# Key-sum reciprocals as logarithm and exponential on ScalarE, and the first layer norm applied by GpSimd from tile 4 on, in a two-layer linear-attention and gated-unit kernel

## The chip, the cores and the metric

One NeuronCore of a Trainium2 chip. Its engines run their own instruction streams side by side: TensorE (PE) multiplies matrices, VectorE (DVE) and ScalarE (ACT) do elementwise work, GpSimd (POOL) does slower elementwise work, and SyncE (SP) issues most of the transfers. The metric is the device time of one execution in microseconds (us); lower is better.

## The reference

The input x has 2048 rows (positions) of 512 values in bf16. Four blocks follow, each added to x after a layer norm: attention, gated unit, attention, gated unit, with the same weights in both rounds.

```
A(x):  q, k, v = split(x @ wqkv), 32 heads of 16
       pq = q @ w_phi[head],  pk = k @ w_phi[head]
       phi = [softmax(p), softmax(-p)]          # 32 features per head, for q and for k
       kv  = sum over positions of phi_k^T v,   z = sum over positions of phi_k
       o   = (phi_q @ kv) / (phi_q . z + 1e-6)
       return o @ wo
B(x):  gate = x @ W_gate, up = x @ W_up          # 1376 columns
       return (relu(gate) * up) @ W_down
x = x + A(ln(x)); x = x + B(ln(x)); x = x + A(ln(x)); x = x + B(ln(x))
```

The softmax runs over 16 values, so for the keys each row of 128 positions needs 64 sums of exponentials (32 heads, two signs) and their 64 reciprocals.

## The kernel before, in words

All of x stays on the chip in `x_sb`, as 16 tiles of 128 rows. The layers are numbered l = 0 to 3: 0 and 2 are attention, 1 and 3 the gated unit. The work of a tile:

- `ln(l, ts)`: for each tile of a group VectorE takes the statistics (`stats`, L558, and their mean and variance `mv`, L559); ScalarE makes `rstd` for the whole group by a logarithm and an exponential (L561, L563); VectorE writes the normalised tile `y` (L572), from a ring of four buffers `p_y`. SyncE then transposes `y` into `yT` by a transfer (L587), or for a few tiles (`PE_Y`) TensorE does, with a copy by ScalarE (L581, L584). In layer 0 the groups are tiles 0, 1, 2, 3, (4, 5), (6, 7), (8 to 11), (12 to 15); elsewhere each tile is its own group.
- `kv_tile(l, t)`: TensorE multiplies `yT` with the composed key weights (L605), ScalarE writes exp(k) and exp(-k) into `phik` (L610), VectorE sums them in groups of 16 into `z`, 64 values (L611), takes the reciprocal `rz` (L613) and multiplies `phik` by it (L614). TensorE makes the values (L623), which ScalarE copies to `vaug` (L626).
- `q_chunk`: queries of four tiles (L639) and their exponentials `expq` (L643). `kv_sums`: the sums over all positions (L659), which need every tile's normalised `phik`; they are masked by VectorE into `kvs` (L667, L670).
- `attn_tile`: product with `kvs` (L692), denominators in `sm` by ScalarE and GpSimd (L706 to L717), VectorE's division and addition (L726, L731, L735), transposed `o`, product with `wo` (L752), addition to x (L755).
- `glu_slab` and `down`: gate and up products (L782), relu on ScalarE (L789), product on VectorE (L790), remainder columns (L810 on), down product (L834, L836), addition to x (L840).

The order of the instructions of each engine is not written by hand. Each `op(...)` names its engine, what it reads and writes, how long it holds its engine (`ii`) and its latency (`lat`), both in ns. `schedule` plans all operations by these figures, in eight rounds of a forward list schedule with priorities from a backward one; `prepare` turns the dependences into semaphore waits, and the engines run the planned orders as fixed queues. A waiting instruction holds up everything behind it on its engine. Buffers come from rings (`Pool`), and the planner also decides which tile has which buffer. When an operation is moved or its figures change, all the orders are planned anew.

ScalarE loads one table of functions at the start, `natural_log_exp_and_others`, and keeps it.

Of the kernel before, what the change touches and what calls it, by code (L numbers as in the profile page):

```python
# [5 lines left out]
FP32 = mybir.dt.float32  # L6
BF16 = mybir.dt.bfloat16
ALU = mybir.AluOpType
ACT = mybir.ActivationFunctionType
# [40 lines left out]
class Program:  # L50
# [8 lines left out]
    def op(self, eng, fn, reads=(), writes=(), parts=(), ii=100.0, lat=None, name="", claims=(), after=(), dma=None, nbytes=0):  # L59


        o = Op()
        o.i, o.eng, o.fn, o.name = len(self.ops), eng, fn, name
        o.ii, o.lat = float(ii), float(ii if lat is None else lat)
        o.dma, o.nbytes = dma, nbytes
        deps, order = set(), set()
        for a in after:
            (order if a.eng == eng else deps).add(a.i)

        def need(d, r):  # L70
            if d is o:
                return
            pe = r.tile is not None and r.tile.pool.psum and d.eng == "pe" and eng == "pe"
            (order if pe else deps).add(d.i)
        for r in reads:
            for w in r.writers:
                need(w, r)
        for r in writes:
            for u in r.writers + r.readers:
                need(u, r)  # L80
        for r in parts:
            for u in r.readers:
                need(u, r)
        for r in reads:
            r.readers.append(o)
        for r in writes:
            r.writers, r.readers = [o], []
        for r in parts:
            r.writers.append(o)
        o.uses = [r.tile for r in dict.fromkeys(list(reads) + list(writes) + list(parts)) if r.tile is not None]  # L90
        o.uses = list(dict.fromkeys(o.uses))
        o.tiles = list(dict.fromkeys(o.uses + list(claims)))
        for t in o.tiles:
            t.users.append(o)
        o.deps, o.order = sorted(deps), sorted(order - deps)
        o.cnt = o.stream = None
        self.ops.append(o)
        return o
# [279 lines left out]
def build_kernel(nc, A_x, A_wqkv, A_w_phi, A_wo, B_x, B_W_gate, B_W_up, B_W_down, out):  # L378
    pr = Program()
    op = pr.op  # L380
# [6 lines left out]
    def sb(name, shape, dt=BF16):  # L387
        return E(nc.sbuf_tensor(name, [P] + list(shape), dt))
# [5 lines left out]
    NT, NS, NC, FC = 16, 4, 4, 10  # L394
    x_sb = sb("x_sb", [NT, 512])
# [8 lines left out]
    mask2 = sb("mask2", [8])  # L404
    eps = sb("eps", [1], FP32)
    kvs = sb("kvs", [8, 144])
    stats, mv, lnv, rstd = sb("stats", [NT, 6], FP32), sb("mv", [NT, 2], FP32), sb("lnv", [NT, 1], FP32), sb("rstd", [NT, 1], FP32)

    p_y = ring("y", 4, [512])
# [24 lines left out]
    def tile(pool, *key):  # L434
        t = Tile(str(key), pool)
        return t, Res(str(key), t)
# [52 lines left out]
    for ic in range(4):  # L489
        t, r = tile(p_hT, "wkn", ic)  # L490
# [25 lines left out]
    for a in range(4):  # L516
        op("dve", lambda e, a=a: e.tensor_tensor(BD[:].rearrange("p c (a f b) -> p c a f b", f=16, b=2)[:, :, a], w128[:].unsqueeze(3).to_broadcast([P, 4, 16, 2]),
                                                 m8[:, 2 * a:2 * a + 2].unsqueeze(1).unsqueeze(1).to_broadcast([P, 4, 16, 2]), ALU.mult),
           reads=[c_w128, c_m8], writes=[c_BD[a]], ii=190, lat=280, name="BD")
# [35 lines left out]
    def ln(l, ts):  # L555

        for t in ts:
            op("dve", lambda e, t=t: e.bn_stats(stats[:, t, :], x_sb[:, t, :]), reads=[res("x", t)], writes=[res("st", t)], ii=600, lat=690, name=f"stat{l}.{t}")  # L558
            op("dve", lambda e, t=t: e.bn_aggr(mv[:, t, :], stats[:, t, :]), reads=[res("st", t)], writes=[res("mv", t)], ii=70, lat=175, name=f"aggr{l}.{t}")  # L559
        a, b = ts[0], ts[-1] + 1  # L560
        op("act", lambda e: e.activation(lnv[:, a:b, :], mv[:, a:b, 1:2], ACT.Ln, bias=eps[:]), reads=[res("mv", t) for t in ts] + [c_eps],  # L561
           writes=[res("lnv", t) for t in ts], ii=186, lat=295, name=f"ln{l}.{a}")
        op("act", lambda e: e.activation(rstd[:, a:b, :], lnv[:, a:b, :], ACT.Exp, scale=-0.5), reads=[res("lnv", t) for t in ts],  # L563
           writes=[res("rstd", t) for t in ts], ii=94, lat=203, name=f"rstd{l}.{a}")
        for t in ts:
            s = t // 4
            if (l, s) not in yT:
                yT[l, s] = Tile(f"yT{l}.{s}", p_yT)
            dst = yT[l, s]
            rr = res("yT", l, t, tile=dst)  # L570
            yt, yr = tile(p_y, "y", l, t)
            op("dve", lambda e, t=t, yt=yt: e.tensor_scalar(yt.ap(), x_sb[:, t, :], mv[:, t, 0:1], rstd[:, t, :], ALU.subtract, ALU.mult),  # L572
               reads=[res("x", t), res("mv", t), res("rstd", t)], writes=[yr], claims=[dst], ii=323, lat=405, name=f"y{l}.{t}")
            c = (t % 4) * 128
            if (l, t) in PE_Y:
                pt, pres = tile(p_ps, "yps", l, t)

                def mm(e, yt=yt, pt=pt):
                    b16 = pt.ap().bitcast(BF16)
                    for k in range(4):  # L580
                        i = e.transpose(b16[:, k * 128:(k + 1) * 128], yt.ap()[:, k * 128:(k + 1) * 128], ident[:])  # L581
                    return i
                op("pe", mm, reads=[yr] + c_id, writes=[pres], ii=230, lat=400, name=f"yT{l}.{t}")
                op("act", lambda e, pt=pt, dst=dst, c=c: e.activation(dst.ap()[:, :, c:c + 128], pt.ap().bitcast(BF16)[:, 0:512].rearrange("p (k n) -> p k n", k=4), ACT.Copy),  # L584
                   reads=[pres], writes=[rr], ii=477, lat=600, name=f"yTcp{l}.{t}")
            else:
                op("sp", lambda e, yt=yt, dst=dst, c=c: e.dma_start_transpose(dst.ap()[:, :, c:c + 128], yt.ap()), reads=[yr], writes=[rr],  # L587
                   dma="tr", nbytes=131072, name=f"yT{l}.{t}")
# [5 lines left out]
    def kv_tile(l, t):  # L594
        src, rr = yT[l, t // 4], res("yT", l, t)
        c0 = (t % 4) * 128
        kt, kr = tile(p_ps, "K", l, t)
        ft, fr = tile(p_ph, "ph", l, t)
        zt, zr = tile(p_z, "z", l, t)
        rt, rzr = tile(p_rz, "rz", l, t)  # L600
        ph[l, t] = (ft, fr)

        def mmk(e):
            for ic in range(4):
                i = e.matmul(kt.ap(), src.ap()[:, ic, c0:c0 + 128], Wkp[:, ic, :], start=(ic == 0), stop=(ic == 3))  # L605
            return i
        kop[l, t] = op("pe", mmk, reads=[rr] + r_wk, writes=[kr], claims=[ft], ii=864, lat=1030, name=f"K{l}.{t}")
        fr2 = [Res("phh", ft), Res("phh", ft)]
        for s in range(2):
            op("act", lambda e, s=s: e.activation(ft.ap()[:, s, :], kt.ap(), ACT.Exp, scale=(1.0, -1.0)[s]), reads=[kr], writes=[fr2[s]], ii=477, lat=600, name=f"expk{l}.{t}")  # L610
        op("dve", lambda e: e.tensor_reduce(zt.ap().rearrange("p (a b) -> p a b", b=2), ft.ap().rearrange("p s (a f b) -> p (s a) b f", f=16, b=2), AX.X, ALU.add),  # L611
           reads=fr2, writes=[zr], ii=1105, lat=1185, name=f"Z{l}.{t}")
        op("dve", lambda e: e.reciprocal(rt.ap(), zt.ap()), reads=[zr], writes=[rzr], ii=420, lat=526, name=f"rZ{l}.{t}")  # L613
        op("dve", lambda e: e.tensor_tensor(ft.ap().rearrange("p s (a f b) -> p (s a) f b", f=16, b=2), ft.ap().rearrange("p s (a f b) -> p (s a) f b", f=16, b=2),  # L614
                                            rt.ap().rearrange("p (a b) -> p a b", b=2).unsqueeze(2).to_broadcast([P, 32, 16, 2]), ALU.mult),
           reads=fr2 + [rzr], writes=[fr], ii=602, lat=695, name=f"norm{l}.{t}")
        vt, vr = tile(p_ps, "V", l, t)
        at, ar = tile(p_va, "va", l, t)
        va[l, t] = (at, ar)

        def mmv(e):
            for ic in range(4):
                i = e.matmul(vt.ap(), src.ap()[:, ic, c0:c0 + 128], wv[:, ic, :], start=(ic == 0), stop=(ic == 3))  # L623
            return i
        op("pe", mmv, reads=[rr, c_wv], writes=[vr], claims=[at], ii=864, lat=1030, name=f"V{l}.{t}")
        op("act", lambda e: e.activation(at.ap()[:, :, 0:128], vt.ap().rearrange("p (c n) -> p c n", c=4), ACT.Copy),  # L626
           reads=[vr] + ([res("va1", i) for i in range(16)] if l == 0 else []), writes=[ar], ii=477, lat=600, name=f"va{l}.{t}")
# [219 lines left out]
    for t in range(NT):  # L847
        kv_tile(0, t)
# [12 lines left out]
    for l in (0, 2):  # L861
# [7 lines left out]
        for s in range(NS):  # L869
# [3 lines left out]
            for t in range(4 * s, 4 * s + 4):  # L873
                down(l + 1, t, last=(l == 2))
                if l == 0:
                    ln(2, [t])
                    kv_tile(2, t)
    pr.schedule(ROUNDS)
    pr.prepare()
# [15 lines left out]


ROUNDS = 8
PE_Y = {(0, 0), (0, 1), (0, 2), (1, 0), (1, 1), (2, 15), (3, 0), (3, 1)}
PE_O = {(0, 0), (0, 1), (2, 0), (2, 1)}

# [42 lines left out]
```

## Time and profile before

| | |
|---|---|
| median of 3 runs | 408.67 us (406.94 to 409.31) |
| profiled execution | 408.02 us |
| its span, first to last instruction | 406.2 us |
| TensorE busy | 386.3 us (95%) |
| VectorE busy | 297.2 us (73%) |
| ScalarE busy | 194.1 us (48%) |
| GpSimd busy | 31.8 us (8%) |

In the profile's lines, L with a number is a line of the kernel, `out<-in` are the program's names for what an operation writes and reads, and xN is a count. A row of a timeline begins with its start and its length in us and ends, in square brackets, with the idle time before it and what ended it. A row of the waits is engine, operation and what it waited for, then total us, times and the longest. A row of the table by stretches has the stretch, its length, and then for TensorE's matmuls, TensorE's weight loads, VectorE, ScalarE and GpSimd the busy us and the number of instructions; behind them stand the clock that was granted to TensorE (1.00 is full speed), the share of the DMA engines and GB/s. A row of a group ends with total us and mean ns of one, then the idle time before.

### The profile page before, as it was taken

Reading aid. Unit: us, or ns where it says so; the run is one execution under the profiler, and the core shown is the slowest. Engines: PE = TensorE matmul, PEld = TensorE weight load, DVE = VectorE, ACT = ScalarE, POOL = GpSimd, SP = SyncE. Lnnn points to the kernel's source line nnn. Section 1 sums busy time; section 2 is a strip of 40 time slices with the busy share of each in tenths; the row PEclk is TensorE's granted clock in tenths of the full one; section 3 lists DMA queues with packets and bytes.
Section 4 is the critical chain, followed back from the end, with each engine's and each line's share of the span. In section 5 each row is a group of like instructions: output and inputs, shape, how many; then the busy total and the mean of one; then the engine's idle time right before and its main releaser. Section 6 shows DMA issues by size and latency. Waiting matters only on the chain.

```text
span 406.2 us, 6510 instructions
## 1 busy us (share of the span) xinstructions
PE 386.3 (95%) x2405; PEld 210.6 (52%) x2405; DVE 297.2 (73%) x635; ACT 194.1 (48%) x567; POOL 31.8 (8%) x119
## 2 busy tenths in 40 slices
PE   5869969999999999999999999989999999999996
PEld 2424645577845454444444466557765544444442
DVE  8989994699888855536499999499988872424424
ACT  4949518966554332323228964985554421203300
POOL 1000001221211000000000000222111200000000
PEclk9969969999999999999999999999999999999999
DMA  8655920133232220101104000013423231100012
GB/s 220 156 80 130 346 71 2 21 57 65 58 59 57 53 46 15 31 15 26 27 2 86 8 0 2 0 34 61 87 44 65 40 65 28 39 27 27 0 40 77
DMA packets 63440, 23.03 MB, mean 57 GB/s; under 512 B 54352, under 2 KB 63408, under 8 KB 63408
## 3 DMA queue, kind: packets, MB, share of 16 engines
q1 hardware_dynamic: 62592, 22.33, 24.3%
q8 instruction: 19, 0.31, 0.3%
q10 hardware_dynamic: 816, 0.28, 0.3%
q14 instruction: 13, 0.11, 0.1%
HBM read 7.91 MB, written 2.10 MB: 25 GB/s over the span
## 4 chain that ended last, share of the span: by engine, by line
PE 66%; DVE 17%; ACT 9%; DMA 3%; issue 2%; POOL 1%
PE pb L782 30%; PE pb L834 17%; ACT expq L643 5%; DVE z L611 4%; PE pb L752 4%; PE pb L605 3%; DVE stats L558 3%; PE pb L659 3%; PE pb L623 2%; DVE phik L614 2%; PE pb L810 2%; DMA oT<-o 2%; PE pb L639 2%; PE pb L836 2%; PE pb L692 2%
## 5 line engine op out<-in xcount | busy, mean ns | idle before, releaser
L789 ACT ACTIVATE gate<-pb 128x512 bf16<-128x512 f32 (+1 forms) x100 | 50.7, 509 | 102.2 <-PE pb L782 101.6
L782 PE MATMUL pb<-yT,Wg 128*128 128x512 bf16 (+1 forms) x400 | 83.6, 337 | 0.0
L782 PE MATMUL pb<-yT,Wu 128*128 128x512 bf16 (+1 forms) x400 | 83.2, 337 | 0.0
L790 DVE TENSOR_TENSOR hT<-gate,pb 128x512 bf16<-128x512 bf16 (+1 forms) x100 | 56.1, 573 | 35.6 <-PE pb L782 35.2
L834 PE MATMUL pb<-Wd,hT 128*128 128x512 bf16 x320 | 74.6, 379 | 0.0
L782 PEld LDWEIGHTS pb<-yT,Wg 128*128 128x128 bf16 x400 | 37.7, 98 | 33.1 <-DVE hT L790 1.3
L782 PEld LDWEIGHTS pb<-yT,Wu 128*128 128x128 bf16 x400 | 38.3, 98 | 28.1 <-DVE hT L790 0.5
L834 PEld LDWEIGHTS pb<-Wd,hT 128*128 128x128 bf16 x320 | 31.2, 98 | 37.9
L840 DVE TENSOR_TENSOR x_sb<-x_sb,pb 128x512 bf16<-128x512 bf16 x32 | 21.8, 681 | 37.3 <-PE pb L836 37.3
L558 DVE BATCH_NORM_STATS2 stats<-x_sb 128x6 f32<-128x512 bf16 x64 | 42.9, 684 | 0.4
L643 ACT ACTIVATE expq<-pb 128x512 bf16<-128x512 f32 x64 | 35.0, 606 | 17.1 <-PE pb L639 17.1
L726 DVE TENSOR_TENSOR t<-pb,sm 128x384 bf16<-128x384 f32 x64 | 32.6, 548 | 7.7 <-POOL sm L717 6.9
L610 ACT ACTIVATE phik<-pb 128x512 bf16<-128x512 f32 x64 | 35.1, 672 | 6.1 <-PE pb L605 6.0
L611 DVE TENSOR_REDUCE z<-phik 128x64 f32<-128x1024 bf16 x32 | 37.2, 1189 | 0.2 <-ACT phik L610 0.2
L561 ACT ACTIVATE lnv<-mv,eps 128x1 f32<-128x1 f32 (+2 forms) x56 | 16.4, 297 | 42.4 <-DVE mv L559 42.3
L605 PE MATMUL pb<-Wkp,yT 128*128 128x512 bf16 x128 | 31.8, 398 | 4.3 <-DMA yT<-y 4.3
L639 PE MATMUL pb<-yT,Wqp 128*128 128x512 bf16 x128 | 31.9, 390 | 1.0 <-DVE t L726 0.8
L752 PE MATMUL pb<-wo,oT 128*128 128x512 bf16 x128 | 32.2, 379 | 0.5 <-DMA oT<-o 0.5
L755 DVE TENSOR_TENSOR x_sb<-x_sb,pb 128x512 bf16<-128x512 bf16 x32 | 21.7, 679 | 14.8 <-PE pb L752 14.7
L713 POOL TENSOR_TENSOR sm<-sm 128x64 f32<-128x64 f32 x32 | 10.5, 329 | 264.2 <-ACT sm L706 264.2
L623 PE MATMUL pb<-wv,yT 128*128 128x512 bf16 x128 | 31.1, 387 | 0.0
L572 DVE TENSOR_SCALAR y<-x_sb,mv,rstd 128x512 bf16<-128x512 bf16 x64 | 25.4, 407 | 4.5 <-ACT rstd L563 2.9
(65 smaller groups left out, 372.7 us busy)
## 6 DMA issues: line engine op xcount, KB each, us to landing
out_dram<-x_sb SPq DMA_DIRECT2D x16, 128.0 KB, 1.7
x_sb<-in_A_x_dram SPq DMA_DIRECT2D x3, 512.0 KB, 5.2
Wg<-in_B_W_gate_dram SPq DMA_DIRECT2D x2, 640.0 KB, 8.0
Wu<-in_B_W_up_dram SPq DMA_DIRECT2D x2, 640.0 KB, 9.0
Wd<-in_B_W_down_dram SPq DMA_DIRECT2D x1, 1280.0 KB, 12.7
yT<-y SPq DMA_TRANSPOSE x56, 2.5
hT<-in_A_wqkv_dram SPq DMA_DIRECT2D x4, 128.0 KB, 3.7
wv<-in_A_wqkv_dram SPq DMA_DIRECT2D x1, 512.0 KB, 5.8
```

The source lines that it names most:

```text
L558: op("dve", lambda e, t=t: e.bn_stats(stats[:, t, :], x_sb[:, t, :]), reads=[res("x", t)], writes=[res("st", t)], ii=600, lat=690, name=f" ...
L605: i = e.matmul(kt.ap(), src.ap()[:, ic, c0:c0 + 128], Wkp[:, ic, :], start=(ic == 0), stop=(ic == 3))
L610: op("act", lambda e, s=s: e.activation(ft.ap()[:, s, :], kt.ap(), ACT.Exp, scale=(1.0, -1.0)[s]), reads=[kr], writes=[fr2[s]], ii=477, la ...
L611: op("dve", lambda e: e.tensor_reduce(zt.ap().rearrange("p (a b) -> p a b", b=2), ft.ap().rearrange("p s (a f b) -> p (s a) b f", f=16, b= ...
L623: i = e.matmul(vt.ap(), src.ap()[:, ic, c0:c0 + 128], wv[:, ic, :], start=(ic == 0), stop=(ic == 3))
L639: i = e.matmul(qt.ap(), Wqp[:, ic, c * 128:(c + 1) * 128], src.ap()[:, ic, :], start=(ic == 0), stop=(ic == 3))
L643: op("act", lambda e, g=g: e.activation(es[g][0].ap(), qt.ap(), ACT.Exp, scale=(1.0, -1.0)[g]), reads=[qr], writes=[es[g][1]], ii=477, lat ...
L752: i = e.matmul(wt.ap(), oT_.ap()[:, c, :], wo[:, c, :], start=(c == 0), stop=(c == 3))
L782: i = e.matmul(pt.ap()[:, 0:n], W[:, ic, fc * 128:(fc + 1) * 128], src.ap()[:, ic, a * 128:b * 128], start=(ic == 0), stop=(ic == 3))
L789: op("act", lambda e: e.activation(st_.ap()[:, 0:n], gt.ap()[:, 0:n], ACT.Relu), reads=[gr], writes=[sr], ii=110 + n * .72, lat=230 + n * ...
L790: op("dve", lambda e: e.tensor_tensor(ht.ap()[:, a * 128:b * 128], st_.ap()[:, 0:n], ut.ap()[:, 0:n], ALU.mult), reads=[sr, ur], writes=[h ...
L834: i = e.matmul(pt.ap(), hT[l, s, fc].ap()[:, c:c + 128], Wd[:, fc, :], start=(fc == 0), stop=False)
```

## The change

Two sets of (layer, tile) pairs choose where two operations run.

`ACT_RZ`: all 16 tiles of layer 0 and the even tiles of layer 2. There the reciprocal of the key sums is no longer VectorE's; ScalarE takes the logarithm of `z` in place and then exp(-log z) into `rz`.

`POOL_Y`: tiles 4 to 15 of layer 0. There `y` is written by GpSimd: a small operation makes `nmr` = -mean * rstd, and a tensor_scalar makes x * rstd + nmr.

```
+    nmr = sb("nmr", [NT, 1], FP32)
...
+            if (l, t) in POOL_Y:
+                op("pool", lambda e, t=t: e.tensor_scalar(nmr[:, t, :], mv[:, t, 0:1], rstd[:, t, :], -1.0, ALU.mult, ALU.mult), reads=[res("mv", t), res("rstd", t)], writes=[res("nmr", t)],
+                   ii=100, lat=170, name=f"nmr{l}.{t}")
+                op("pool", lambda e, t=t, yt=yt: e.tensor_scalar(yt.ap(), x_sb[:, t, :], rstd[:, t, :], nmr[:, t, :], ALU.mult, ALU.add), reads=[res("x", t), res("nmr", t), res("rstd", t)],
+                   writes=[yr], claims=[dst], ii=1000, lat=1050, name=f"yp{l}.{t}")
+            else:
               op("dve", lambda e, t=t, yt=yt: e.tensor_scalar(yt.ap(), x_sb[:, t, :], mv[:, t, 0:1], rstd[:, t, :], ALU.subtract, ALU.mult),
                  reads=[res("x", t), res("mv", t), res("rstd", t)], writes=[yr], claims=[dst], ii=323, lat=405, name=f"y{l}.{t}")
...
-        op("dve", lambda e: e.reciprocal(rt.ap(), zt.ap()), reads=[zr], writes=[rzr], ii=420, lat=526, name=f"rZ{l}.{t}")
+        if (l, t) in ACT_RZ:
+            lz = Res("lz", zt)
+            op("act", lambda e: e.activation(zt.ap(), zt.ap(), ACT.Ln), reads=[zr], writes=[lz], ii=150, lat=260, name=f"lZ{l}.{t}")
+            op("act", lambda e: e.activation(rt.ap(), zt.ap(), ACT.Exp, scale=-1.0), reads=[lz], writes=[rzr], ii=150, lat=260, name=f"rZa{l}.{t}")
+        else:
+            op("dve", lambda e: e.reciprocal(rt.ap(), zt.ap()), reads=[zr], writes=[rzr], ii=420, lat=526, name=f"rZ{l}.{t}")
...
+ACT_RZ = {(0, t) for t in range(16)} | {(2, t) for t in range(0, 16, 2)}
+POOL_Y = {(0, t) for t in range(4, 16)}
```

More of the change, by code (lines that the diff above doesn't have):

```diff
@@ L571, in ln @@
             yt, yr = tile(p_y, "y", l, t)
-            op("dve", lambda e, t=t, yt=yt: e.tensor_scalar(yt.ap(), x_sb[:, t, :], mv[:, t, 0:1], rstd[:, t, :], ALU.subtract, ALU.mult),
+            if (l, t) in POOL_Y:
[4 more added lines that the diff above has]
+            else:
+              op("dve", lambda e, t=t, yt=yt: e.tensor_scalar(yt.ap(), x_sb[:, t, :], mv[:, t, 0:1], rstd[:, t, :], ALU.subtract, ALU.mult),
                reads=[res("x", t), res("mv", t), res("rstd", t)], writes=[yr], claims=[dst], ii=323, lat=405, name=f"y{l}.{t}")
```

## The prediction

> **What bounds the kernel now.** I read the page's busy parts and slices first, then the list of waits, then a table by stretches, then the timelines of the stretches where TensorE stands still.
>
> ```profile
> span 406.2 us, 6510 instructions
> PE 386.3 (95%) x2405; PEld 210.6 (52%) x2405; DVE 297.2 (73%) x635; ACT 194.1 (48%) x567; POOL 31.8 (8%) x119
> ...
> PE   5869969999999999999999999989999999999996
> DVE  8989994699888855536499999499988872424424
> PEclk9969969999999999999999999999999999999999
> ```
>
> The average says TensorE (95%). The slices, 10.2 us each, show the exception: in slices 3 and 6 (about 20 to 30 and 51 to 61 us) TensorE falls to 6 tenths, its granted clock to 6 or 7 tenths, while VectorE stands at 9. The waits of 12 to 66 us name what TensorE waited for:
>
> ```profile
> PE pb L605 <- DMA yT<-y: 4.3, 1, 4.3
> PE pb L659 <- DVE phik L614: 3.3, 1, 3.3
> ```
>
> And the table by stretches (length, then busy time and count of each engine, granted clock, DMA) gives the price:
>
> ```profile
> 19.13:23.41 4.28, 0.00 (x0) 0.00 (x0) 4.28 (x16) 2.19 (x7) 0.00 (x0) 0.87 0.15 31
> 23.41:28.56 5.15, 5.15 (x13) 1.84 (x14) 3.69 (x7) 1.68 (x3) 0.00 (x0) 0.50 0.88 106
> 28.56:50.83 22.27, 22.27 (x149) 11.97 (x147) 22.27 (x35) 17.36 (x33) 0.00 (x0) 0.99 0.77 224
> 50.83:54.17 3.34, 0.00 (x1) 0.01 (x1) 3.34 (x6) 0.00 (x0) 0.00 (x0) 0.83 0.67 209
> 54.17:61.30 7.13, 7.13 (x44) 4.93 (x45) 6.29 (x11) 1.73 (x4) 0.00 (x0) 0.60 0.00 0
> 66.00:200.00 134.00, 132.24 (x814) 72.58 (x812) 95.44 (x218) 62.22 (x210) 14.99 (x48) 1.00 0.21 39
> 200.00:300.00 100.00, 97.96 (x714) 59.02 (x713) 87.47 (x182) 65.65 (x196) 10.17 (x33) 1.00 0.16 32
> ```
>
> TensorE idles 4.28 and 3.34 us in the first phase, and after each hole it runs at clock 0.50 and 0.60. At full clock a 512-column matmul takes 0.216 us and a key-sum one 0.058:
>
> ```profile
> 30.72 1.73 PE pb L605 x8
> 43.67 1.40 PE pb L659 x24
> ```
>
> The 13 matmuls behind the first hole would take 2.81 us, not 5.15: 2.34 lost. Behind the second, 32 x 0.058 + 12 x 0.216 = 4.45, not 7.13: 2.68 lost. So hole 1 costs 4.28 + 2.34 = 6.6 us and hole 2 costs 3.34 + 2.68 = 6.0: 12.6 us together. From 66 us on TensorE's work fills the time (132.24 of 134 us, 97.96 of 100) and I treat it as one block that moves. Those 12.6 us are what a change to this phase can win.
>
> **The change part by part.** The timeline of VectorE around the holes:
>
> ```profile
> 15.49 4.83 DVE L558 BATCH_NORM_STATS2 stats<-x_sb 128x6 f32<-128x512 bf16 x8
> ...
> 20.52 1.35 DVE L572 TENSOR_SCALAR y<-x_sb,mv,rstd 128x512 bf16<-128x512 bf16 x4
> 21.78 0.37 DVE L559 BATCH_NORM_AGGREGATE mv<-stats 128x2 f32<-128x6 f32 x4
> ...
> 27.61 0.41 DVE L572 TENSOR_SCALAR y<-x_sb,mv,rstd 128x512 bf16<-128x512 bf16 x1 [1.46 <-DMA yT<-y]
> 27.94 0.96 DVE L613 RECIPROCAL rz<-z 128x64 bf16<-128x64 f32 x2
> 28.81 1.16 DVE L611 TENSOR_REDUCE z<-phik 128x64 f32<-128x1024 bf16 x1
> ...
> 35.66 2.49 DVE L614 TENSOR_TENSOR phik<-phik,rz 128x1024 bf16<-128x1024 bf16 x4
> ...
> 59.24 1.23 DVE L614 TENSOR_TENSOR phik<-phik,rz 128x1024 bf16<-128x1024 bf16 x2
> ```
>
> *Taken from VectorE.* Start to start, two reciprocals take 28.81 - 27.94 = 0.87 us, so 0.435 each; four y take 21.78 - 20.52 = 1.26, so 0.315 each. First phase: 16 x 0.435 = 6.96 and 12 x 0.315 = 3.78. The wait of 1.46 us for a free y buffer goes with the y operations to GpSimd, behind which nothing is queued there before the attention. Together 12.2 us off a VectorE that is busy until 59.24 + 1.23 = 60.47: its part could end at 48.3.
>
> *Hole 1.* The four y at 20.52 are tiles 4 to 7. Their scale was ready long before:
>
> ```profile
> 16.52 0.39 ACT L563 ACTIVATE rstd<-lnv 128x2 f32<-128x2 f32 x2
> ...
> 20.92 2.44 DMA yT<-y
> 23.41 1.89 PE pb L605 x4
> ```
>
> Ready at 16.91, they stood in VectorE's queue behind eight statistics. On GpSimd, tile 4 starts at 16.91. The price of a 512-element tensor_scalar there is in no row. Nearest rows:
>
> ```profile
> L464 POOL MEMSET hr<- 128x512 bf16 x2 | 1.0, 538 | 0.0
> L717 POOL TENSOR_TENSOR sm<-sm 128x64 f32<-128x64 f32 x32 | 10.3, 321 | 22.5 <-ACT sm L716 22.5
> ...
> L714 POOL TENSOR_TENSOR sm<-sm x32: 251/252/498, 66.5 to 322.8; 128x32 f32<-128x32 f32 x32
> ```
>
> Below, 0.54 us (a 512-element write without a read); above, the slope of the two-input operation, (0.321 - 0.252)/32 = 2.2 ns an element, so 0.252 + 480 x 0.0022 = 1.29 us. I take 1.05, the planner's figure in the diff, between these ends: its figures for the two operations just shown, 0.322 and 0.252 in the code, are what the rows measure. The small nmr operation: between 0.10 (its planner figure) and 0.25, taken as 0.17. Tile 4's y is then done at 16.91 + 0.17 + 1.05 = 18.13, its transpose 2.44 us later at 20.6, against 23.4: hole 1 shrinks from 4.28 to some 1.5 us and, being short, I expect no slow clock behind it. Won: 2.8 + 2.3 = 5.1 of 6.6 (at the upper price 4.8). Afterwards GpSimd delivers a tile each 1.22 us (1.5 at the upper price); TensorE takes 8 x 0.216 = 1.73 for a tile's keys and values, so GpSimd isn't the pace. SyncE's queue sees the same twelve transposes, earlier, and the weight loads behind them earlier too.
>
> The Trainium skill's GPSIMD Engine Reference, section 3.1, gives 769 ns for a 512-element loop and in 4.1 says to keep elementwise work on VectorE, though one-input operations run roughly at line rate; no row here shows either. By 0.77 instead of 1.05 the total below would be 0.3 us better.
>
> *The reciprocal on ScalarE.* The nearest rows are the attention's logarithm and exponential of 32 elements, then the next instruction:
>
> ```profile
> 66.75 0.23 ACT L715 ACTIVATE sm<-sm 128x32 f32<-128x32 f32 x1
> 67.01 0.23 ACT L716 ACTIVATE sm<-sm 128x32 f32<-128x32 f32 x1
> 67.15 0.58 ACT L643 ACTIVATE expq<-pb 128x512 bf16<-128x512 f32 x1
> ```
>
> A pair holds ScalarE 67.15 - 66.75 = 0.40 us (lower end, two issues of 0.14, 0.28; upper, two full 0.23 and twice the elements, 0.55). Sixteen pairs are 6.4 us (4.5 to 8.8). Cover: from 19.13 to 61.30 ScalarE is busy 2.19 + 1.68 + 17.36 + 0 + 1.73 = 23.0 of 42.2 us. If that cover were gone, all 6.4 would fall on the path. It is thinnest in 28.56 to 50.83, where 4.9 us are free. The pair adds a wait: the logarithm stands at the head of ScalarE's queue until VectorE's sum is done, with the next key exponentials and value copies behind it, and TensorE's buffers behind those. VectorE in turn must wait about 0.5 us for the normalisation, or do another tile's sum between.
>
> *Hole 2.* The key sums waited for the last normalisations. With VectorE's end at 48.3 TensorE becomes as late: its work of 23.41 to 61.30, 37.89 us, holds 3.34 idle and 5.02 of slow clock, so 29.5 net; begun at 20.6, it ends at 50.1. ScalarE, with 6.4 more, is near there too. Three engines that end within about 2 us of each other don't mesh without waits, so I take 3.5 of hole 2's 6.0 us as won; the ends are 0 and 6.0.
>
> *Second layer.* Eight reciprocals leave VectorE (8 x 0.435 = 3.5 us) and eight pairs come to ScalarE (3.2 us; it has 34 of 100 free). TensorE idles only 2.04 us in 200 to 300, so between -1 (a reordered plan) and +1.5; I take 0.5.
>
> Sum: 5.1 + 3.5 + 0.5 = 9.1 us, ends 2 and 14. The profiled execution took 408.02 us, 1.82 above its span and 0.65 below the median of 408.67. Span 406.2 - 9.1 = 397.1, time 398.9; I say 399.0.
>
> **The rivals.**
> (a) *The gain is mostly lost to the shared queueing of VectorE and GpSimd.* GpSimd's 32-element add takes 0.252 us, up to 0.498 when it begins while VectorE adds two SBUF tensors:
>
> ```profile
> 91.24 0.42 DVE L735 TENSOR_TENSOR o<-t 128x512 bf16<-128x512 bf16 x1
> 91.27 0.49 POOL L714 TENSOR_TENSOR sm<-sm 128x32 f32<-128x32 f32 x1
> ```
>
> It finished only after the VectorE operation did. If that also holds the other way round, a normalisation (two SBUF inputs) that meets a y on GpSimd waits up to 1.05 us. GpSimd is in y for 12 x 1.05 = 12.6 us of about 30, so some 7 of 16 meet it: 3.5 us at half a y each, 7.4 at a whole. VectorE then ends 4.8 to 8.7 earlier and not 12.2. Won: about 4 to 8 us, less meshing; time near 404. Against it: the first normalisations run at 35.66, when GpSimd's y would be done (16.91 + 12 x 1.22 = 31.6). The SBUF page of the Trainium skill ("SBUF — State Buffer", Who interferes with whom) states this as an exclusive lock that VectorE's two-input operations and GpSimd's reads contend for; the row above agrees for GpSimd's side, and no row shows VectorE's.
> (b) *The change does not do what it says.* All orders are planned anew; a new order that puts y or key sums as badly as the batch of eight statistics at 15.49 gives a hole of 4 to 6 us back, twice: time within 2 us of 408.
> (c) *Slower: ScalarE's queue blocks.* Each of the 16 logarithms waits at the head of the queue for a sum that runs late, and the key exponentials behind it wait too. VectorE's saving is 12.2; a stall of 0.8 us per tile (16 x 0.8 = 12.8) eats it, and 1.1 per tile gives 17.6 and 5 us slower, 413. For it: ScalarE was 78% busy in 28.56 to 50.83. Against: late in the phase ScalarE has slack to absorb it, 10.40 us of idle before its first query exponential:
>
> ```profile
> 59.56 4.26 ACT L643 ACTIVATE expq<-pb 128x512 bf16<-128x512 f32 x8 [10.40 <-PE pb L639]
> ```
>
> **How the numbers follow.** Forecast (395 to 403.5) 0.60; (a) 0.18; (b) 0.11; (c) 0.08; better than 395, both holes gone, 0.03. Half a per cent, 2.0 us, is about what a measurement of this kernel can tell from no change. Faster by more: 0.60 + 0.18 + 0.03 and a little of (b), 0.82; same 0.10; slower 0.08. The range leaves out (c), the far end of (b) and the best: 393 to 407.
>
> **What would show it.** Right: yT's wait at 19 us under 2 us, granted clock 1.0 from 21 to 30; VectorE's last first-layer normalisation near 50 us; the first expq near 50, not 59.56; GpSimd's y near 1.05 us; the stretch from the first attention to the end as long as before. Wrong: a new wait of key exponentials behind the logarithm, GpSimd's y over 2.5 us (then it is slower than TensorE's 1.73 and sets the pace), normalisations over 1 us each, or a new hole after 66 us.

## The result, and the profile after

The changed kernel takes 397.59 us (median of 4 runs, 396.22 to 398.57) against 407.81 before (4 runs, 406.3 to 409.31): ratio 0.9747, 95% interval 0.9695 to 0.9799. Run again beside its variants it gave 398.63 us and 0.9773 (0.9749 to 0.9796). The forecast was 399.0.

The page of the changed kernel, with the lines that answer to those shown of before:

```profile
span 396.3 us, 6545 instructions
...
PE 383.5 (97%) x2405; PEld 209.8 (53%) x2405; DVE 283.4 (72%) x599; ACT 199.2 (50%) x615; POOL 44.7 (11%) x143
...
PE   6979999999999999999999999999999999999996
DVE  8898957998889636545699993799888962433424
PEclk9999999999999999999999999999999999999999
```

Of TensorE's slices 3 and 6 (here 9.9 us each), 6 tenths before, the third now reads 7 and the sixth 9, and the clock's row reads 9 throughout. The line numbers have moved: key product L605 is now L612, key sums L659 are L671, the sums `z` L611 are L618, reciprocal on ScalarE L622 and L623, normalisation L614 is L626, `y` on GpSimd L576, the first attention product L692 is L704. The waits of the changed kernel, 12 to 66 us:

```profile
POOL nmr L574 <- ACT rstd L564: 13.8, 2, 12.8
...
PE pb L612 <- DMA yT<-y: 2.5, 2, 1.6
...
ACT z L622 <- DVE z L618: 2.1, 2, 1.2
POOL y L576 <- DMA yT<-y: 2.0, 2, 1.9
DVE z L618 <- ACT rz L623: 2.0, 2, 1.3
```

TensorE's wait for normalisations, 3.3 us before, is gone; its wait for transposed `y` is 2.5 us in two pieces and not 4.3 in one. New are the round trips: ScalarE waits 2.1 us for sums, VectorE 2.0 us for the reciprocals to free a buffer of sums. The table by stretches (columns as before):

```profile
14.47:20.71 6.24, 6.24 (x43) 3.15 (x40) 4.65 (x7) 6.24 (x18) 2.85 (x7) 1.00 0.35 77
20.71:21.61 0.90, 0.00 (x1) 0.01 (x1) 0.90 (x6) 0.90 (x4) 0.90 (x2) 1.00 0.29 58
21.61:26.10 4.49, 4.49 (x20) 1.79 (x20) 4.49 (x10) 4.41 (x13) 3.39 (x8) 1.00 0.70 92
26.10:27.67 1.57, 0.00 (x0) 0.00 (x0) 1.57 (x2) 1.04 (x5) 0.00 (x0) 1.00 0.53 86
27.67:55.80 28.13, 28.13 (x224) 16.81 (x225) 24.39 (x35) 22.61 (x63) 6.17 (x9) 1.00 0.70 203
55.80:190.00 134.20, 132.54 (x827) 73.59 (x826) 94.85 (x219) 62.71 (x213) 14.71 (x48) 1.00 0.20 39
```

From 27.67 us TensorE doesn't stand still until the attention, and in that stretch both VectorE (24.39 of 28.13) and ScalarE (22.61) have slack. The roles have changed: from 27.67 us on the phase is TensorE's now.

The best single mark of the phase is the start of the first attention product, from TensorE's timeline. Before:

```profile
64.90 1.16 PE L692 MATMUL pb<-kvs,expq 128*128 128x144 bf16 x16
```

After:

```profile
55.80 1.16 PE L704 MATMUL pb<-kvs,expq 128*128 128x144 bf16 x16
```

It comes 9.10 us earlier; the span is 9.9 us shorter. So what lies behind it took 406.2 - 64.90 = 341.3 us and takes 396.3 - 55.80 = 340.5: a block that moved.

### The profile page after: what moved, and what is told of

It is laid out like the page before. It is cut to its first block, busy times and chain, and to the rows that moved or that the text cites. A ratio compares the mean times of both kernels' runs of the same rounds, so it can differ in the third digit from the quotient of the medians.

```text
span 396.3 us, 6545 instructions
## 1 busy us (share of the span) xinstructions
PE 383.5 (97%) x2405; PEld 209.8 (53%) x2405; DVE 283.4 (72%) x599; ACT 199.2 (50%) x615; POOL 44.7 (11%) x143
## 4 chain that ended last, share of the span: by engine, by line
PE 79%; ACT 9%; DVE 7%; POOL 2%; DMA 1%; issue 1%; POOLq 0%
PE pb L794 33%; PE pb L846 17%; PE pb L635 6%; PE pb L612 6%; ACT expq L655 5%; PE pb L764 4%; PE pb L671 4%; PE pb L822 2%; PE pb L651 2%; PE pb L704 2%; PE pb L848 2%; DVE stats L559 1%; DMA yT<-y 1%; ACT sm L718 1%; DVE t L738 1%; DVE y L579 1%
## 5 line engine op out<-in xcount | busy, mean ns | idle before, releaser
L618 DVE TENSOR_REDUCE z<-phik 128x64 f32<-128x1024 bf16 x32 | 37.5, 1206 | 3.6 <-ACT rz L623 2.0
L612 PE MATMUL pb<-Wkp,yT 128*128 128x512 bf16 x128 | 30.7, 386 | 2.5 <-DMA yT<-y 2.5
L651 PE MATMUL pb<-yT,Wqp 128*128 128x512 bf16 x128 | 30.8, 380 | 1.0 <-DVE t L738 0.8
L579 DVE TENSOR_SCALAR y<-x_sb,mv,rstd 128x512 bf16<-128x512 bf16 x52 | 21.1, 409 | 3.0 <-ACT rstd L564 2.9
```

Source lines behind the costliest of these rows:

```text
L651: i = e.matmul(qt.ap(), Wqp[:, ic, c * 128:(c + 1) * 128], src.ap()[:, ic, :], start=(ic == 0), stop=(ic == 3))
```

## The experiments

All are timed in five rounds against the kernel before on the same chip.

**The two parts apart.** First the reciprocals alone, and y alone:

```
-POOL_Y = {(0, t) for t in range(4, 16)}
+POOL_Y = set()
```

> Only the reciprocals move to ScalarE (16 in layer 0, 8 in layer 2); every y stays on VectorE. Theory (two holes, each with its own cause): VectorE is 7.0 us shorter in the first phase, so hole 2 closes (6.0 us); hole 1 mostly stays, because the y of tiles 4 to 7 stay in VectorE's queue with the statistics of tiles 8 to 15: 1 to 3 us of it won. Time 4 to 7 us below before, about 402. Rival (either part alone is enough, since the plan is made anew anyway): the same time as the whole change, about 398.

```
-ACT_RZ = {(0, t) for t in range(16)} | {(2, t) for t in range(0, 16, 2)}
+ACT_RZ = set()
```

> Only y of tiles 4 to 15 moves to GpSimd; the reciprocals stay on VectorE. Theory: hole 1 shrinks as in the whole change (about 4 us won), but VectorE is only 5.2 us shorter (3.8 of y, 1.5 of a wait) and still ends last, near 55 us, so hole 2 stays: total gain at most these 5.2 us, 2 to 5 us, time 403 to 406. Rival: same time as the whole change, about 398.

The reciprocals alone: 399.44 us, ratio 0.9814 (0.9794 to 0.9833), 7.9 us below the 407.33 of before, timed beside it; y alone: 401.68 us, 0.9875 (0.9849 to 0.9900), 5.6 us. Together they would give 13.5 where the whole gives about 10. The reciprocals alone come close to it: their ratio is 0.0041 to 0.0067 above the two of the whole change, some 1.7 to 2.7 us, and the intervals just touch. What moving y adds to them is that little. VectorE's timeline, its last normalisation (or last run of them) before the attention, with the reciprocals alone:

```profile
53.14 0.69 DVE L626 TENSOR_TENSOR phik<-phik,rz 128x1024 bf16<-128x1024 bf16 x1 [1.01 <-ACT rz L623]
```

and with y alone, followed by TensorE's two holes there:

```profile
54.38 1.21 DVE L626 TENSOR_TENSOR phik<-phik,rz 128x1024 bf16<-128x1024 bf16 x2
```

```profile
20.71 1.04 PE L612 MATMUL pb<-Wkp,yT 128*128 128x512 bf16 x4 [1.08 <-DMA yT<-y]
...
49.30 2.02 PE L671 MATMUL pb<-vaug,phik 128*128 128x129 bf16 x32 [3.22 <-DVE phik L626]
```

With the reciprocals alone hole 2 is gone, as the theory said, though TensorE still idles 2.93 and 0.70 us for transposed y; its first attention product starts at 55.83 us, where the whole change has 55.80. With y alone hole 1 is down to pieces of 1.08 us at most and hole 2 stays at 3.22, as the theory said. But its key sums behind the hole run at 2.02/32 = 0.063 us and not 0.114 (3.65/32 before): the slow clock is not the price of every hole of this length. (This trace is of the fastest of the six executions, 400.28 us at a granted clock of 1.00; the other five show 0.992 to 0.998, so some of them may have paid it.) Both parts gave more than expected (7.9 where 4 to 7 stood, 5.6 where 2 to 5 stood).

**The order alone.** The kernel before, with VectorE's batch of statistics bound behind the four y:

```
-... writes=[res("st", t)], ii=600, lat=690, name=f"stat{l}.{t}")
+... writes=[res("st", t)], ii=600, lat=690, name=f"stat{l}.{t}", after=[yop[0, k] for k in range(4, 8)] if l == 0 and t >= 8 else [])
```

> The kernel before, every operation on its old engine; only the order is bound: statistics of tiles 8 to 15 come after the y of tiles 4 to 7 on VectorE. Theory: hole 1 closes or shrinks, but VectorE's work is the same and it still ends near 60 us, so hole 2 grows by what hole 1 loses: time within 2 us of before, 406 to 409; only the slow clock behind hole 1 could be saved. Rival (the order was at fault, not VectorE's load): 4 to 6 us faster, 402 to 404.

407.56 us, ratio 1.0006 (0.9987 to 1.0025): no change. TensorE's waits in it, 9 to 66 us:

```profile
PE pb L659 <- DVE phik L614: 6.1, 2, 4.0
...
PE pb L605 <- DMA yT<-y: 2.2, 3, 1.3
```

Hole 1 went from 4.3 to 2.2 us, in three pieces with full-speed matmuls behind them, and hole 2 grew from 3.3 to 6.1. VectorE's last normalisation:

```profile
59.46 1.22 DVE L614 TENSOR_TENSOR phik<-phik,rz 128x1024 bf16<-128x1024 bf16 x2
```

It ends at 60.68, against 60.47 before. This shows that hole 1 by itself, as far as it was closed here, was worth nothing: while VectorE's load sets the end of the phase, what TensorE gains at 20 us it waits for at 50.

**The load put back.** The changed kernel with a reciprocal of a constant on VectorE for each tile, unused:

```
+        dum = []
+        if l == 0:
+            dum = [op("dve", lambda e: e.reciprocal(dz[:, 1, :], dz[:, 0, :]), reads=[res("dz0")], writes=[res("dz1")], ii=420, lat=526, name=f"dR{l}.{t}", after=[zop])]
...
-           reads=fr2 + [rzr], writes=[fr], ii=602, lat=695, name=f"norm{l}.{t}")
+           reads=fr2 + [rzr], writes=[fr], ii=602, lat=695, name=f"norm{l}.{t}", after=dum)
```

> The changed kernel with 16 extra reciprocals on VectorE in layer 0, one per tile between its sum and its normalisation, of a constant and into a buffer nobody reads: the 7.0 us of VectorE load that the change took away are put back, without the reciprocal's place in the chain. Theory (VectorE's load in the first phase is what counted): the time goes back to that of the kernel with y alone moved, 3 to 5 us slower than the changed kernel, about 401 to 403, with a wait of the key sums for normalisations. Rival (the shorter chain or the new order counted): within 1 us of the changed kernel.

404.49 us, ratio 0.9905 (0.9870 to 0.9941), 5.9 us above the changed kernel's 398.63: more than expected, and 2.8 us above y alone (401.68), which has the same reciprocals on VectorE. TensorE's timeline has hole 2 and the slow clock again:

```profile
49.33 6.54 PE L676 MATMUL pb<-vaug,phik 128*128 128x129 bf16 x64 [3.91 <-DVE phik L631]
61.86 1.16 PE L709 MATMUL pb<-kvs,expq 128*128 128x144 bf16 x16
```

The 64 key sums take 6.54 us; in the changed kernel the same 64 take 3.86 and wait for nothing:

```profile
45.48 3.86 PE L671 MATMUL pb<-vaug,phik 128*128 128x129 bf16 x64
```

With the order experiment this shows that VectorE's load in the first phase counts: taken away, hole 2 closes, put back, it opens (3.91 us, 3.22 with y alone), though the reciprocal's place in the chain is still ScalarE's. The start of the first attention product is 4.5 us later than with y alone (57.32), and most of that is the clock: 2.7 us of slow key sums here, and some 1.5 us of slow first matmuls (10.6 to 14.0 us), of which the trace of y alone has neither. What is left, like ScalarE's longer waits for sums (6.2 us, 2.1 in the changed kernel), can come of the new plan; no run separates that. What follows the first attention product is here 402.4 - 61.86 = 340.5 us, as in the changed kernel.

**ScalarE's cover.** Two extra exponentials per tile double the pair's price. The first try read z and so disturbed the buffers:

```
+                op("act", lambda e: e.activation(dz[:, 0, :], zt.ap(), ACT.Exp, scale=-1.0), reads=[lz], writes=[res("dz", 0)], ...)
+                op("act", lambda e: e.activation(dz[:, 1, :], zt.ap(), ACT.Exp, scale=-1.0), reads=[lz], writes=[res("dz", 1)], ...)
```

> The changed kernel with two extra 64-element exponentials per tile on ScalarE in layer 0, into a buffer nobody reads: the price of the moved reciprocal there is doubled (16 x 2 x 0.14 to 0.2, 4.5 to 6.4 us more). Theory (TensorE is the bound of the first phase now, ScalarE has some 4 to 5 us left in it): 0 to 3 us slower than the changed kernel's 398. Rival (ScalarE's queue already sets the end): all of it, 4.5 to 6.4 us slower.

408.12 us, ratio 1.0029 (1.0002 to 1.0057): all of the gain gone, far more than either theory. The waits of 9 to 70 us show why it doesn't answer the question:

```profile
DVE z L619 <- ACT dz L626: 10.9, 2, 9.0
```

The extra readers were queued late and kept the four `z` buffers; VectorE's sums waited 9.0 us at one time for a free one. Mended, with a constant as input and a fixed place between logarithm and reciprocal:

```
+            for i in range(2 if l == 0 else 0):
+                prev = op("act", lambda e, i=i: e.activation(dz[:, 1 + (2 * t + i) % 8, :], dz[:, 0, :], ACT.Exp, scale=-1.0), reads=[res("dz0")], ..., after=[prev])
```

> The doubled ScalarE price again, with the flaw of the first try mended: there the extra exponentials read z and were queued late, so they held the four z buffers and VectorE's sums waited 8.98 us for one. Here the two extra exponentials of a tile read a constant and stand between its logarithm and its reciprocal, so they hold no buffer. ScalarE's load rises by 16 x 0.29 = 4.6 us, the chain of each tile by 0.3 us. Theory (ScalarE has slack left): 0 to 3 us slower than the changed kernel's 398, 398 to 401. Rival (ScalarE's queue is as full as TensorE's): 4.6 us or more slower, 403 or later.

396.27 us, ratio 0.9728 (0.9700 to 0.9755): no slower at all. ScalarE's table by stretches shows the extra work inside its slack (26.42 of 28.13 us where the changed kernel has 22.61; the stretch here reaches past the first attention product at 54.13, and up to that ScalarE is busy 24.95 of 26.46):

```profile
27.67:55.80 28.13, 27.60 (x229) 16.48 (x231) 23.82 (x33) 26.42 (x97) 2.61 (x7) 1.00 0.65 194
```

So the price of the pair was hidden, and twice that price as well, though little slack is left then. The first try shows what late readers of a four-buffer ring can cost; the mended one took away both the reading of `z` and the late place, so it does not tell which of the two mattered.

**The lock between VectorE and GpSimd.** Twenty extra operations on GpSimd beside the normalisations:

```
+    for i in range(20):
+        lastp = [op("pool", lambda e: e.tensor_scalar(junk[:], wv[:, 0, :], rstd[:, 15, :], nmr[:, 15, :], ALU.mult, ALU.add), reads=[c_wv, res("rstd", 15), res("nmr", 15)],
+           writes=[res("junk")], ii=750, lat=800, name=f"noise{i}", after=lastp)]
```

> The changed kernel with 20 more 512-element tensor_scalars on GpSimd behind its last y, written to a buffer nobody reads, so that they run beside VectorE's normalisations. It measures the lock by itself. If GpSimd alone waits (as the last y, 2.23 us and not 0.76): normalisations keep 0.68 us, the extra operations beside them take up to 2 us or more, and the time is unchanged within 1 us. If VectorE waits as well: normalisations grow to 1 to 1.4 us each, 4 to 8 us on VectorE, and the kernel is 2 to 6 us slower than the changed one.

398.21 us, ratio 0.9773 (0.9751 to 0.9796), beside 398.63 of the changed kernel: no change. GpSimd's row in it, and VectorE's normalisations (minimum, median, maximum in ns):

```profile
L864 POOL TENSOR_SCALAR junk<-wv,rstd,nmr x20: 769/772/2118, 32.4 to 54.2; 128x512 bf16<-128x512 bf16 x20
```

```profile
L627 DVE TENSOR_TENSOR phik<-phik,rz x32: 626/681/1091, 30.1 to 238.2; 128x1024 bf16<-128x1024 bf16 x32
```

Both sides wait. Five normalisations in a run took 3.74 us here and 3.09 in the changed kernel:

```profile
41.41 3.74 DVE L627 TENSOR_TENSOR phik<-phik,rz 128x1024 bf16<-128x1024 bf16 x5
```

```profile
42.99 3.09 DVE L626 TENSOR_TENSOR phik<-phik,rz 128x1024 bf16<-128x1024 bf16 x5
```

A run of normalisations loses up to 0.8 us (a pair took 2.10 us in place of 1.28), and GpSimd up to 1.35 us on one operation. The 16 normalisations of the first layer took about 1.9 us longer in all, not the 4 to 8 of the second theory, and VectorE has more slack than that. In the changed kernel only GpSimd's last y met any, beside a run of three:

```profile
31.77 1.88 DVE L626 TENSOR_TENSOR phik<-phik,rz 128x1024 bf16<-128x1024 bf16 x3
```

```profile
31.91 2.23 POOL L576 TENSOR_SCALAR y<-x_sb,rstd,nmr 128x512 bf16<-128x512 bf16 x1 [0.17 <-DMA yT<-y]
```

**What is left of hole 1.** Statistics in pairs, and then also five y buffers and the measured prices in the plan:

```
-    for g in ([0], [1], [2], [3], [4, 5], [6, 7], [8, 9, 10, 11], [12, 13, 14, 15]):
+    for g in ([0], [1], [2], [3], [4, 5], [6, 7], [8, 9], [10, 11], [12, 13], [14, 15]):
```

> The changed kernel with the statistics of tiles 8 to 15 in groups of two and not of four (two more logarithm and exponential pairs on ScalarE). Theory: with hole 2 closed TensorE is the bound, and what is left of hole 1 (0.90 and 1.57 us) is on the path; the second wait comes of GpSimd having no ready tile until the scale of the group of four, at 22.6 us. Groups of two give it one about 1.5 us earlier: 1 to 2 us faster than the changed kernel. Rival (VectorE or ScalarE still sets the end): the same time within 0.5 us.

> As the last one, with five y buffers and not four, and the planner's figures of GpSimd's operations as measured (0.75 and 0.245 us for 1.0 and 0.1). Theory: GpSimd's waits for a buffer (1.87 us once) don't reach TensorE once tiles are ready earlier, so within 1 us of the last one. Rival (the buffers, not the statistics, held the second wait): another 1 to 1.5 us faster.

398.69 us, 0.9777 (0.9754 to 0.9799), and 397.39 us, 0.9758 (0.9735 to 0.9781), against 0.9773 of the changed kernel timed beside them. The first theory is not borne out: 1 to 2 us were expected and none came. The second version is 1.3 us faster than the first, the size that its rival named, but the intervals overlap and nothing is settled. TensorE still waits 1.8 us and 2.5 us for transposed y in them: the waits only moved. The changed kernel again, beside them:

> The changed kernel once more, beside its variants. In its first profile the first key and value matmuls (10.9 to 14.3 us) took 0.43 us each and not 0.22, about 1.7 us, though nothing was changed there. Theory: the state of the clock at the start differs from execution to execution; here they take 0.22 us and the first attention product starts near 54 us, not 55.8. Rival: it belongs to this kernel; then 0.43 us again. Time 396 to 399 either way.

398.63 us. The first matmuls were slow again (1.91 us for four, as in the first profile), so the theory is wrong and its rival came. The first attention product does start at 53.97, span 394.7, but for another reason: in this profile the second piece of hole 1 (1.57 us) is missing, so that piece is not a fixed part of the kernel.

**The second layer.**

```
-ACT_RZ = {(0, t) for t in range(16)} | {(2, t) for t in range(0, 16, 2)}
+ACT_RZ = {(0, t) for t in range(16)}
```

> The whole change without its layer-2 part (ScalarE reciprocals in layer 0 only). Theory: TensorE idles only 1 to 2 us in that part with or without it, so within 1 us of the whole change (397 to 399). Rival: the second layer carries a part of the gain as large as its 3.5 us of VectorE work; then about 401.

```
+ACT_RZ = {(0, t) for t in range(16)} | {(2, t) for t in range(16)}
+POOL_Y = {(0, t) for t in range(4, 16)} | {(2, t) for t in range(15)}
```

> The changed kernel with more of the second layer moved: y of tiles 0 to 14 of layer 2 to GpSimd, and all 16 reciprocals of layer 2 to ScalarE. VectorE is relieved of another 15 x 0.315 + 8 x 0.435 = 8.2 us between 190 and 260 us. Theory (TensorE fills that stretch, 98.58 of 100 us): within 1 us of the changed kernel. Rival (VectorE's load counts there as in the first phase): 3 us or more faster.

Without its layer-2 part 398.65 us, 0.9797 (0.9774 to 0.9819); with more of it 396.64 us, 0.9757 (0.9724 to 0.9789). Both intervals overlap those of the changed kernel. By the ratios leaving that part out costs 1.0 to 2.0 us and moving more of it lies between 0.7 us faster and 0.4 slower, none of it clear of the noise, though 8.2 us more were taken from VectorE there.

## Why the prediction was right, by its own steps

The forecast was 9.1 us off the span; it was 9.9, and 9.0 to 10.2 between the medians. As forecast, the first query exponential comes near 50 us (50.25) and not at 59.56. The terms fared differently, and that their sum came within 0.8 us is in part luck: hole 2 gave 2.5 more than taken, hole 1 0.5 less, the block behind 0.3 more, and 1.6 were lost at a place that the sum does not have.

- *Hole 1, 5.1 us forecast of 6.6.* The hole's price was put too low. The 2.34 us of slow clock count the 13 matmuls up to 28.56 us, but in TensorE's timeline before the slow ones go on behind that, and 16 matmuls take from 23.41 to 29.70:

```profile
23.41 1.89 PE L605 MATMUL pb<-Wkp,yT 128*128 128x512 bf16 x4 [4.29 <-DMA yT<-y]
25.09 1.91 PE L623 MATMUL pb<-wv,yT 128*128 128x512 bf16 x4
26.80 3.06 PE L605 MATMUL pb<-Wkp,yT 128*128 128x512 bf16 x8
29.70 1.03 PE L623 MATMUL pb<-wv,yT 128*128 128x512 bf16 x4
```

  That is 6.29 us where 16 x 0.216 = 3.46 would do, so 2.83 lost and 7.1 for the hole. Idle 4.28 became 0.90 + 1.57 and the slow clock went: 1.81 + 2.83 = 4.6 won. GpSimd began at 17.86 and not at 16.91. That comes, as far as the rows show, of the slow first matmuls, below: ScalarE's key exponentials wait for them, and the scale stands behind some of these in its queue. Where the first matmuls run at full speed, in the kernel without the layer-2 part, GpSimd begins at 16.27:

```profile
16.27 0.50 POOL L574 TENSOR_SCALAR nmr<-mv,rstd 128x1 f32<-128x1 f32 x2 [11.25 <-ACT rstd L564]
```

- *Hole 2, 3.5 us forecast of 6.0.* All 6.0 were won. I expected three engines that end together not to mesh. They did: TensorE runs through from 27.67 us, and VectorE and ScalarE keep slack beside it (24.39 and 22.61 of 28.13 us).
- *A loss that was not forecast.* The first eight value and key matmuls, 10.93 to 14.25 us, took 3.32 us and not 8 x 0.216 = 1.73, so 1.6 were lost, described below. 4.6 + 6.0 - 1.6 = 9.0, against the 9.10 us of the mark. This is the account of one profile. The second profile of the changed kernel has slow first matmuls too, and yet reaches the mark at 53.97; without the layer-2 part, at full speed, it comes at 53.87, with more idle time for transposed y (2.0 us, 0.9 there). So a part of that loss can stand in for waits.
- *Second layer, 0.5 forecast.* The block behind the mark is 0.8 us shorter, but with the reciprocals alone, whose layer 2 is planned with the same moves of reciprocals, it is 397.9 - 55.83 = 342.1, longer than before. A new plan shifts it by that much; the term is not shown.
- *The form of the sum was wrong.* I added hole 1 and hole 2 as if each could be won alone. The order experiment shows that hole 1 alone is worth 0 (1.0006). The right reading is one bound: VectorE's end of the phase, 60.47, with the slow clock behind it, and under it TensorE's own work. It came out right because the change lowered the load as well. The low end of 2 us does not follow either: the lower ends given are 4.8 + 0 - 1 = 3.8. (In the reading of the slices, VectorE's row has 8 and not 9 in slice 3.)
- *VectorE's end, 48.3 forecast, was 53.8.* The load taken away was right, but VectorE now waits, once for ScalarE's key exponentials and three times for the reciprocals made there:

```profile
16.06 1.22 DVE L618 TENSOR_REDUCE z<-phik 128x64 f32<-128x1024 bf16 x1 [1.61 <-ACT phik L617]
...
30.64 1.22 DVE L618 TENSOR_REDUCE z<-phik 128x64 f32<-128x1024 bf16 x1 [1.27 <-ACT rz L623]
...
34.35 1.22 DVE L618 TENSOR_REDUCE z<-phik 128x64 f32<-128x1024 bf16 x1 [0.69 <-ACT rz L623]
...
53.11 0.69 DVE L626 TENSOR_TENSOR phik<-phik,rz 128x1024 bf16<-128x1024 bf16 x1 [1.24 <-ACT rz L623]
```

  1.61 + 1.27 + 0.69 + 1.24 = 4.8 of the 5.5 us.
- *GpSimd's price, 1.05 + 0.17 taken,* was 0.745 + 0.235, from two of each start to start in its timeline (18.33 to 19.82, and 17.86 to 18.33):

```profile
17.86 0.49 POOL L574 TENSOR_SCALAR nmr<-mv,rstd 128x1 f32<-128x1 f32 x2 [12.85 <-ACT rstd L564]
18.33 1.51 POOL L576 TENSOR_SCALAR y<-x_sb,rstd,nmr 128x512 bf16<-128x512 bf16 x2
19.82 0.49 POOL L574 TENSOR_SCALAR nmr<-mv,rstd 128x1 f32<-128x1 f32 x2
20.29 1.51 POOL L576 TENSOR_SCALAR y<-x_sb,rstd,nmr 128x512 bf16<-128x512 bf16 x2
```

  The Trainium skill's GPSIMD Engine Reference, section 3.1, gives 769 ns for a 512-element loop; the rows here have 762 ns for most of the y, and 769 at least for the extra operations. Taking the planner's figure over it was the worse choice, and harmless.
- *ScalarE's pair, 0.40 taken,* holds it 0.14 to 0.15 us per operation when other work stands between the two, so 0.29, near the lower end (each start to the next in ScalarE's timeline). The cover was there, as the doubled pair shows.

```profile
18.84 0.31 ACT L622 ACTIVATE z<-z 128x64 f32<-128x64 f32 x1
18.98 0.65 ACT L638 ACTIVATE vaug<-pb 128x512 bf16<-128x512 f32 x1
19.46 0.32 ACT L623 ACTIVATE rz<-z 128x64 bf16<-128x64 f32 x1
19.61 1.14 ACT L546 ACTIVATE Wqp<-pb 128x512 bf16<-128x512 f32 x2
```

- *Rivals.* (a) exists, both ways, but met one operation in the changed kernel and cost nothing even when provoked. (b) and (c) did not come; (c)'s waits of the logarithm are 2.1 us in all, in ScalarE's slack. That (b) stayed away was not certain in advance: the plan was made anew in every kernel here, and the block behind the mark ranged over 340.5 to 342.3.

No version clearly beats the changed kernel: five buffers (0.9758), more of layer 2 (0.9757) and even the extra exponentials (0.9728) all overlap its 0.9747 and 0.9773 in their intervals. Nor does the gain hang on one lucky order: seven kernels that take both loads off VectorE in the first layer, most of them with plans of their own, take 396.3 to 398.7 us, and only the one whose late readers kept the `z` buffers does not.

## What to carry to other kernels

Two holes of an engine under one loaded neighbour are one loss, not two: ask what the neighbour's total load permits, and test a repaired hole by looking whether the next one grew. Load moved to idle engines pays until the next engine's own work is the floor; in layer 2, where TensorE's work fills the time, another 8.2 us of relief were worth nothing that could be measured. When adding a reader to a small ring of buffers, ask when it will let go of its buffer, and not only how long it runs: exponentials of 0.15 us that read the ring late cost 10 us, the same number that read a constant, in a fixed place, cost none.

## What the runs showed of the hardware that was not expected

The granted clock in the records can miss slow matmuls. In the changed kernel the stretch of the first matmuls reads 1.00, and yet four of them take 1.71 us from start to start (12.64 - 10.93), 0.43 each, where full speed is 0.216:

```profile
10.93:14.47 3.54, 3.54 (x14) 1.44 (x13) 3.52 (x11) 1.22 (x3) 0.00 (x0) 1.00 0.96 269
```

```profile
10.93 1.91 PE L635 MATMUL pb<-wv,yT 128*128 128x512 bf16 x4
12.64 1.77 PE L612 MATMUL pb<-Wkp,yT 128*128 128x512 bf16 x4
```

The Trainium skill's page "TensorE: Matmul & The Clock Gate", Part 1, warns that the clock's trace events are unreliable; this row agrees. Both profiles of the changed kernel show the slow start, and the one without the layer-2 part, with the same first layer, does not (0.86 us for the four, start to start). Six of the fourteen profiles have it, all of kernels with both parts of the change, and six kernels' profiles with one part or both do not; what sets it stays open.

GpSimd held off by VectorE can wait for several back-to-back normalisations, and not only for one: its y took 2.23 us beside a run of three (1.88 us together), and 0.76 alone. It need not wait for the end of the run. In the kernel with twenty extra operations, in the run of five from 41.41 us, one extra operation took 2.12 us and ended at 44.01, and the fourth normalisation, beside its end, took 1.09 and not 0.68:

```profile
41.89 2.12 POOL L864 TENSOR_SCALAR junk<-wv,rstd,nmr 128x512 bf16<-128x512 bf16 x1
```

```profile
43.46 1.09 DVE L627 TENSOR_TENSOR phik<-phik,rz 128x1024 bf16<-128x1024 bf16 x1
```

So VectorE waits in its turn, 0.65 us over this run. The Trainium skill's "SBUF — State Buffer", Who interferes with whom, has the lock and that the order of issue decides who blocks; the rows agree with both, on VectorE's side too: the run's first normalisation, begun at 41.41 while an extra operation was under way (41.02 to 41.79), took 0.92 and not 0.68.
